# Summing the squares of the weights on VectorE before their norm products, and a rearranged last unit

## The chip, the cores and the metric

The kernel runs on one core of one Trainium2 chip. The metric is the device time of one execution in microseconds. The kernel before takes 677.63 us (median of 3 runs, 677.48 to 678.36).

## The reference

An attention over 32 memory slots feeds a feed-forward layer of two weight matrices. Cut to what matters:

```python
a = softmax(phi, axis=sequence)                     # 8 batches, 8 heads, 576 positions, 32 slots
k_m, v_m = a^T @ k, a^T @ v                         # 32 x 64 for each head
attn = softmax(q @ k_m^T / 8)                       # 576 x 32 for each head
x = (attn @ v_m)                                    # 4608 tokens x 512
h = x @ w_in                                        # 512 x 2048
out = (h - tanh(h)) @ w_out                         # 2048 x 512
```

The inputs q and k are drawn with standard deviation 20, the others as the reference has them.

## The kernel before

The fast path (`split_path`) holds w_in and w_out as pairs of float16 tiles, a high and a low part, and replaces h - tanh(h) by a short polynomial that is right for small h. Whether the inputs are small enough is checked on the chip: `stat` collects a number for each weight block and each column, `check` (L899) compares them with windows, `check_all` (L915) counts the results into `c["bad"]`, and at the end of the program every engine loads this flag (L1061) and branches (L1062) over `wide_path`, a slow general version that doesn't run here.

**Units and steps.** The 4608 tokens are 18 units of 256; the 2048 hidden columns are four blocks. After a start that is written out by hand, the loop at L844 goes through steps, one for each pair of unit and block; step number sl is 4 x unit + block and runs from 18 to 71. A step issues, in this order: the first product `mm1` of its unit and block (L540, tile hs) with its squaring on ScalarE (L547); `g1` on VectorE (L555), which reads hs; the words of list 0; `g1_square` on ScalarE (L560); on VectorE the four sums of `a_forms` (L587) for the step before and `g2` (L564); the second product `mm2_blocks` (L666 and L673) of two steps earlier; the words of list 1; `g2_high` on ScalarE (L569) and `g3` on GpSimd (L574); the words that were put off (`due`); `evict`, when a unit has been finished; the words of list 2. `in_order` (L889) then ties every instruction to the one before it on its engine, so that each engine works in exactly this order.

**The words.** Lists 0, 1 and 2 of a step are what stands ahead of ";", behind ";" and behind "|" in the entries of PLAN (L797), PLAN3 and PLAN_C (L809). For each batch PLAN places the attention work: among others "S" (scores, L246, with two transposes on VectorE, L256), "P" (`att_p`: 24 matmuls, L492, and a copy on ScalarE, L505) and "PL" (`att_pl`: the low half of that product on VectorE, L510). The entries of the batches go into a step's lists first (L817), those of PLAN_C after them (L820). The last batch has S in list 0 of steps 55 and 56, and P with PL in list 0 of steps 58, 59, 60 and 62.

**The norm products.** The check needs the sum of squares of each column of w_in and w_out. "SI" and "SO" square 2048 columns of float16 weights on ScalarE (L422, L438) into a tile of four blocks of 512 columns. "NI" and "NO" multiply these by a column of ones on TensorE: for each of four groups of 128 columns, four matmuls of one column accumulate the four blocks (L429, L447), and ScalarE copies the result (L434, L451). There are eight such products, NI0 to NI3 and NO0 to NO3, in list 2 of steps 32, 40, 48, 55, 57, 59, 61 and 63.

**PSUM.** The pool ps_a has one buffer, and all of its tiles have the tag "pa": the attention products (psc, pp), the norm products (pni, pno) and the check's product (pgood) take it in turn. hs and the sums x have their own banks, and the two output tiles o[0] and o[1] of a unit (pool ps_o) one buffer each: a new unit's first product into o[0] (L666) waits until `evict` has read the old one.

**The end of a unit.** `evict` (L715) puts the unit's output together on VectorE (L722 to L725, then L733 for each half of the tokens) and stores it (L734). For the last unit the second half goes in two pieces of 256 columns (L730), stored from two queues (L731).

Of the kernel before, what the change touches and what calls it, by code (L numbers as in the profile page):

```python
# [8 lines left out]
F32 = mybir.dt.float32  # L9
# [5 lines left out]
ALU = mybir.AluOpType  # L15
# [3 lines left out]
P = 128  # L19
# [4 lines left out]
NUNIT = B * S // UT  # L24
# [15 lines left out]
CW = (  # L40
    0.33333331252017, -0.13333128520786, 0.053934788850892, -0.021660115374759,
    0.0082189218977914, -0.0025104593252184, 0.000420695493864,
)
# [1 line left out]


V_WIN = (2.0 ** -12, 0.0025)
WI_WIN = (2.0 ** -6, 1.5)
WO_WIN = (2.0 ** -6, 3.5)
N_F1 = 32  # L50


# [260 lines left out]
def split_path(ctx, tc, c, ins, out):  # L313
    nc = tc.nc
# [6 lines left out]
    ps_a = ctx.enter_context(tc.tile_pool(name="ps_a", bufs=1, space=PSUM))  # L321
# [4 lines left out]
    wout_hi = const.tile([P, 16, DM], F16, name="wout_hi")  # L326
# [59 lines left out]
    def low(p):  # L386
        lo = low_of(p)
        for i in range(2):
            nc.vector.scalar_tensor_tensor(
                lo[:, i], tfs[p][i], S_W, his[p][:, i], op0=ALU.mult, op1=ALU.subtract  # L390
            )
# [28 lines left out]
    def squares_in(fb):  # L420
        acc["q", fb] = big.tile([P, 4, 512], F16, tag="q" if fb < 3 else "e", name=f"sqi{fb}", bufs=2 if fb < 3 else 1)
        nc.scalar.activation(acc["q", fb], win_hi[:, :, 512 * fb : 512 * fb + 512], AF.Square, scale=S_Q)  # L422

    def norms_in(fb):
        sq = acc.pop(("q", fb))
        pa = ps_a.tile([P, 2, 512], F32, tag="pa", name=f"pni{fb}")
        for k in range(4):
            for pr in range(4):
                nc.tensor.matmul(  # L429
                    pa[:, 0, k : k + 1], sq[:, pr, P * k : P * k + P], c["ones16"],  # L430
                    start=(pr == 0), stop=(pr == 3),
                )
        o = N_F1 + 2 * B + 4 * fb
        nc.scalar.activation(stat[:, o : o + 4], pa[:, 0, 0:4], AF.Copy, scale=(S_W * S_Q) ** -2)  # L434

# [4 lines left out]
    def norms_out(part):  # L440
        if part == 0:
            acc["n"] = big.tile([P, 4, 4], F32, tag="wn", name="wn", bufs=1)
        sq = acc.pop(("q", part))
        pa = ps_a.tile([P, 2, 512], F32, tag="pa", name=f"pno{part}")
        for k in range(4):
            for i in range(4):
                nc.tensor.matmul(  # L447
                    pa[:, 0, k : k + 1], sq[:, i, P * k : P * k + P], c["ones16"],
                    start=(i == 0), stop=(i == 3),
                )  # L450
        nc.scalar.activation(acc["n"][:, :, part], pa[:, 0, 0:4], AF.Copy, scale=(S_W * S_Q) ** -2)  # L451
        if part == 3:
            o = N_CHECK - 4
            nc.vector.tensor_reduce(stat[:, o : o + 4], acc["n"], axis=AX.X, op=ALU.add)
# [146 lines left out]
    acc = {}  # L601
# [50 lines left out]
    def mm2_blocks(u, fb, first, last):  # L652

        f, gg = gs.pop((u, fb))
        x = acc["x"]
        if first:
            acc[u] = [ps_o.tile([P, DM], F32, tag=f"o{i}", name=f"o{u}{fb}{i}") for i in range(2)]  # L660
        o = acc[u]
        ws = (wout_hi, wout_lo)

        def main(th):
            for k in range(4):
                nc.tensor.matmul(  # L666
                    o[th], gg[:, 0, k, P * th : P * th + P], wout_hi[:, 4 * fb + k, :], start=(first and k == 0), stop=False
                )

        def prod(dst, a, b, new=False, end=False):  # L670
            for kk in range(2):
                for n in range(2):
                    nc.tensor.matmul(  # L673
                        dst, a(1 - n, kk), b(n, kk), start=(new and kk == 0 and n == 0), stop=(end and kk == 1 and n == 1)
                    )

        def ab(th, kh):
            return lambda n, kk: gg[:, n, 2 * kh + kk, P * th : P * th + P]

        def af(i):  # L680
            return lambda n, kk: f[:, n, i, kk]

        def bb(kh, nh):
            return lambda n, kk: ws[n][:, 4 * fb + 2 * kh + kk, 256 * nh : 256 * nh + 256]

        def bf(i):
            return lambda n, kk: bts[i][:, n, fb, kk]

        lo, hi = slice(0, 256), slice(256, 512)
        m1 = (x[:, 0, lo], ab(0, 0), bb(0, 0), first)  # L690
        m2 = (o[0][:, lo], ab(0, 1), bb(1, 0))
        m3 = (o[0][:, hi], af(0), bb(1, 1))
        m4 = (o[1][:, lo], ab(1, 1), bf(3))
        m5 = (x[:, 0, hi], af(2), bf(0))
        m6 = (x[:, 1, lo], af(3), bf(1), first)
        m7 = (x[:, 1, hi], af(1), bf(2))
        if not last:
            main(0)
            main(1)
            for m in (m2, m4, m1, m5, m6, m7, m3):  # L700
                prod(*m)
            return
        sc = 1.0 / (S_G * S_W)
        ra, rb = (big.tile([P, 3, 256], F32, tag="pr", name=f"r{u}{i}") for i in range(2))
        for m, end in ((m1, False), (m5, True), (m6, False), (m7, True)):
            prod(*m, end=end)
        nc.scalar.activation(ra[:, 1], x[:, 0, lo], AF.Copy, scale=sc)
        nc.scalar.activation(rb[:, 2], x[:, 0, hi], AF.Copy, scale=sc)
        for th, ms in ((0, (m2, m3)), (1, (m4,))):
            main(th)  # L710
            for m in ms:
                prod(*m, end=m is ms[-1])
        acc["evict"] = (u, ra, rb)

    def evict():  # L715
        if "evict" not in acc:
            return
        u, ra, rb = acc.pop("evict")
        x, o, t0 = acc["x"], acc[u], u * UT
        sc = 1.0 / (S_G * S_W)  # L720
        lo, hi = slice(0, 256), slice(256, 512)
        nc.vector.scalar_tensor_tensor(ra[:, 0], x[:, 1, lo], sc, ra[:, 1], op0=ALU.mult, op1=ALU.add)  # L722
        nc.vector.scalar_tensor_tensor(rb[:, 0], x[:, 1, hi], sc, ra[:, 0], op0=ALU.mult, op1=ALU.add)
        nc.vector.tensor_tensor(ra[:, 2], ra[:, 0], rb[:, 2], op=ALU.add)
        nc.vector.tensor_tensor(rb[:, 1], rb[:, 0], rb[:, 2], op=ALU.add)  # L725
        for th, r in ((0, ra[:, 1:3]), (1, rb[:, 0:2])):
            r = r.rearrange("p a x -> p (a x)")
            if u == NUNIT - 1 and th == 1:
                for cs, q in ((hi, nc.sync), (lo, nc.scalar)):
                    nc.vector.scalar_tensor_tensor(r[:, cs], o[th][:, cs], sc, r[:, cs], op0=ALU.mult, op1=ALU.add)  # L730
                    q.dma_start(out[t0 + P :, cs], r[:, cs])  # L731
                continue
            nc.vector.scalar_tensor_tensor(r, o[th], sc, r, op0=ALU.mult, op1=ALU.add)  # L733
            nc.sync.dma_start(out[t0 + P * th : t0 + P * th + P, :], r)  # L734
# [16 lines left out]
    def two(f, g, *x):  # L751
# [15 lines left out]
        "AT": lambda b, t: att.soft_turn(b, st[b], t), "AS": lambda b, t: att_split(b, t, nc.gpsimd), "ASv": lambda b, t: att_split(b, t, nc.vector),  # L767
        "Z": warm, "P": att_p, "PL": att_pl, "H": mm1, "a": lambda u, fb: two(g1, g1_square, u, fb), "b": lambda u, fb: two(g2, g2_high, u, fb), "c": lambda u, fb: g3(u, fb, nc.gpsimd), "cv": lambda u, fb: g3(u, fb, nc.vector), "PLp": att_pl_pe,
        "T": lambda x, y: conv(10 * x + y), "L": lambda x, y: low_pool(10 * x + y), "Lv": lambda x, y: low(10 * x + y), "Lp": lambda x, y: low_pe(10 * x + y),
        "G": b_form, "SI": squares_in, "NI": norms_in, "SO": squares_out, "NO": norms_out,  # L770
        "GG": lambda: check(tc, c, big), "GX": lambda: check_all(tc, c, ps_a),
        "M": lambda u, fb: mm2(u, fb, fb in (0, 2), fb in (1, 3)), "R": load_part, "OP": save_part, "O": save,
    }
# [14 lines left out]
    first = len(nc.cur_bb.bb.instructions)  # L788
    for word in START.split():
        if ":" in word:  # L790
            k, tag = word.split(":")
# [15 lines left out]
    )  # L807

    PLAN_C = (  # L809
# [5 lines left out]
    )  # L815
    tasks = {}
    for b in range(3, B):  # L817
# [64 lines left out]
    a_forms(*forms.pop())  # L882
    for u, fb in queue:
        mm2_blocks(u, fb, fb == 0, fb == NFB - 1)
    evict()
    in_order(tc, first)

# [11 lines left out]
def check(tc, c, big):  # L899
# [4 lines left out]
    o = N_F1  # L904
    for n, (lo, hi) in ((2 * B, V_WIN), (DF // P, WI_WIN), (DM // P, WO_WIN)):
        s, g = stat[:, o : o + n], good[:, o : o + n]
# [134 lines left out]
def tile_kernel(ctx: ExitStack, tc: tile.TileContext, qt, kva, kvt, pha, phx, w_in, w_out, out):  # L1041
    nc = tc.nc
    ins = dict(qt=qt, kva=kva, kvt=kvt, pha=pha, phx=phx, w_in=w_in, w_out=w_out)
    const = ctx.enter_context(tc.tile_pool(name="const", bufs=1))
    c = {}
# [12 lines left out]
    nc.gpsimd.memset(c["beta"], BETA)  # L1058
    with ExitStack() as inner:
        split_path(inner, tc, c, ins, out)  # L1060
    bad = nc.values_load(c["bad"][0:1, 0:1], min_val=0, max_val=1)  # L1061
    with tc.If(bad > 0):  # L1062
        with ExitStack() as inner:
            wide_path(inner, tc, c, ins, out)

# [38 lines left out]
```

## Time and profile before

| | |
|---|---|
| median of 3 runs | 677.63 us |
| the profiled execution | 677.7 us |
| its span, first to last instruction | 675.9 us |
| TensorE matmuls busy | 640.8 us (95%) |
| VectorE busy | 510.7 us (76%) |
| ScalarE busy | 375.7 us (56%) |
| GpSimd busy | 256.1 us (38%) |
| norm products of w_in (L429) | 64 matmuls, 334.0 to 534.1 us |
| norm products of w_out (L447) | 64 matmuls, 549.7 to 599.5 us |
| squarings for them (L422, L438) | 8 on ScalarE, 1.89 us each |

PE is TensorE's matmuls, PEld its weight loads, DVE VectorE, ACT ScalarE, POOL GpSimd, SP the engine that issues most transfers; a q behind a name is an engine's instruction queue. A row of the timeline has start, duration, engine, line, operation, output<-input, shapes and a count of merged instructions; in square brackets stands how long the engine was idle before it and what ended that. The chain of waits is the work that ended last, followed back from the end. A row of the busy time by stretch has the stretch, its length, the busy time of PE, PEld, DVE, ACT and POOL (with instruction counts), the granted TensorE clock, the share of the DMA engines and GB/s.

### The profile page before, as it was taken

How to read it: one execution, taken by the hardware profiler on the slowest of the kernel's cores; microseconds unless marked ns; L12 is line 12 of the kernel's file. 1: busy time of each engine (PE TensorE's matmuls, PEld its weight loads, DVE VectorE, ACT ScalarE, POOL GpSimd, SP SyncE). 2: the span in 40 equal slices, each digit the busy share in tenths (PEclk: the TensorE clock that was granted, in tenths of full speed). 3: DMA queues.
4: the chain of work that ended last, by engine and by line, in shares of the span. 5: the costliest groups of instructions: out<-in, count | busy, mean ns of one | idle time of the engine just before them, and what ended most of it. 6: DMA issues, size and time to landing. Idle time of an engine off the chain costs nothing.

```text
span 675.9 us, 15441 instructions
## 1 busy us (share of the span) xinstructions
PE 640.8 (95%) x6628; PEld 447.2 (66%) x6628; DVE 510.7 (76%) x784; ACT 375.7 (56%) x506; POOL 256.1 (38%) x170
## 2 busy tenths in 40 slices
PE   4678989999999999999999999999999999999996
PEld 1336465565646567786767777777777777887874
DVE  4688999989655577965697868886888586867673
ACT  1558477765533355653565455646554587666541
POOL 0032623423111334452345344534453555455521
PEclk9979999999999999999999999999999999999999
DMA  9679663422313132214331523152415224234201
GB/s 342 265 280 363 244 180 125 172 99 86 119 63 107 60 125 72 66 62 176 102 106 42 192 80 121 49 192 68 134 49 190 72 103 121 72 118 137 77 32 37
DMA packets 26428, 86.16 MB, mean 127 GB/s; under 512 B 2928, under 2 KB 3184, under 8 KB 25584
## 3 DMA queue, kind: packets, MB, share of 16 engines
q1 hardware_dynamic: 25056, 82.87, 35.9%
q10 hardware_dynamic: 1296, 2.23, 0.9%
q8 instruction: 54, 0.88, 0.6%
q14 instruction: 22, 0.18, 0.1%
HBM read 73.55 MB, written 11.53 MB: 126 GB/s over the span
## 4 chain that ended last, share of the span: by engine, by line
PE 69%; DVE 6%; ACT 1%; DMA 1%; issue 0%; SPq 0%; DVEq 0%; ACTq 0%
PE hs L540 19%; PE o L666 12%; PE x L673 12%; PE o L673 9%; PE o L617 7%; PE h L540 2%; PE pp L492 2%; PE pkv L194 2%; DVE f L587 2%; PE o1h L617 2%; DVE h L555 1%; DVE h L564 1%; PE psc L246 1%; DMA kv<-in_kva_dram 1%; ACT u L547 1%
## 5 line engine op out<-in xcount | busy, mean ns | idle before, releaser
L574 POOL TENSOR_TENSOR g<-h,g 128x1024 f16<-128x1024 f32 x64 | 145.2, 2268 | 321.8 <-ACT g L569 212.5
L540 PEld LDWEIGHTS <-ph 128*128 128x128 f16 x2304 | 176.6, 98 | 21.9 <-issue 6.5
L540 PE MATMUL hs<-ah,ph 128*128 128x256 f16 (+3 forms) x1088 | 145.8, 248 | 0.0
L555 DVE SCALAR_TENSOR_TENSOR h<-hs,u 128x1024 f32<-128x1024 f32 x52 | 63.5, 1221 | 96.3 <-ACT u L547 96.3
L569 ACT ACTIVATE g<-h 128x1024 f16<-128x1024 f32 x72 | 76.0, 1055 | 94.8 <-DVE h L564 86.0
L540 PE MATMUL hs<-al,ph 128*128 128x256 f16 (+3 forms) x544 | 122.2, 248 | 0.0
L560 ACT ACTIVATE u<-u,beta 128x1024 f32<-128x1024 f32 x72 | 82.6, 1148 | 61.5 <-DVE h L555 61.0
L666 PE MATMUL o<-wout_hi,g 128*128 128x512 f16 x416 | 100.7, 380 | 1.5 <-DVE r L733 1.5
L564 DVE SCALAR_TENSOR_TENSOR h<-u,h 128x1024 f32<-128x1024 f32 x72 | 89.0, 1236 | 5.0 <-ACT u L560 4.6
L673 PEld LDWEIGHTS <-f 128*128 128x128 f16 x832 | 81.3, 98 | 9.5
L617 PEld LDWEIGHTS <-g 128*128 128x128 f16 x480 | 45.7, 98 | 59.4 <-issue 4.1
L547 ACT ACTIVATE u<-hs 128x1024 f32<-128x1024 f32 x52 | 53.0, 1019 | 53.1 <-PE hs L540 53.1
L617 PE MATMUL o<-wout_hi,g 128*128 128x512 f16 x256 | 78.6, 380 | 1.3 <-DVE g L574 0.8
L673 PE MATMUL x<-bt,f 128*128 128x256 f16 x624 | 76.6, 273 | 0.0
L673 PEld LDWEIGHTS <-g 128*128 128x128 f16 x624 | 60.5, 98 | 21.7 <-issue 0.8
L666 PEld LDWEIGHTS <-g 128*128 128x128 f16 x416 | 38.4, 98 | 48.5 <-issue 13.6
L587 DVE TENSOR_TENSOR f<-g 128x512 f16<-128x512 f16 x104 | 59.7, 614 | 3.9 <-POOL g L574 3.4
L540 PE MATMUL h<-ah,ph 128*128 128x256 f16 (+2 forms) x448 | 55.8, 243 | 0.0
L540 PE MATMUL h<-al,ph 128*128 128x256 f16 (+2 forms) x224 | 48.0, 242 | 1.0 <-DVE al L483 1.0
L617 PE MATMUL o<-wout_lo,g 128*128 128x512 f16 x128 | 48.6, 380 | 0.0
L510 DVE SCALAR_TENSOR_TENSOR ph<-pp,ph 128x1024 f16<-128x1024 f32 x30 | 36.5, 1216 | 1.9 <-ACT ph L505 1.7
L505 ACT ACTIVATE ph<-pp 128x1024 f16<-128x1024 f32 x32 | 32.5, 1016 | 4.0 <-PE pp L492 4.0
(134 smaller groups left out, 945.6 us busy)
## 6 DMA issues: line engine op xcount, KB each, us to landing
kv<-in_kva_dram SPq DMA_DIRECT2D x20, 516.0 KB, 4.0
q<-in_qt_dram SPq DMA_DIRECT2D x16, 576.0 KB, 4.1
chk<-in_w_in_dram SPq DMA_DIRECT2D x16, 512.0 KB, 5.2
chk<-in_w_out_dram SPq DMA_DIRECT2D x16, 512.0 KB, 3.4
out_dram<-r SPq DMA_DIRECT2D x25, 256.0 KB, 2.6
kv<-in_kva_dram SPq DMA_DIRECT2D x6, 1032.0 KB, 10.6
raws<-in_w_in_dram SPq DMA_DIRECT2D x12, 512.0 KB, 6.0
raw<-in_w_out_dram SPq DMA_DIRECT2D x12, 512.0 KB, 6.7
```

The lines of the kernel that those rows point to most:

```text
L510: nc.vector.scalar_tensor_tensor(pl, pa, S_P / (S_V * S_W), ph, op0=ALU.mult, op1=ALU.subtract)
L540: nc.tensor.matmul(hp[:, k, tu : tu + w], px[:, g, cs], d[ax][:, g, ta : ta + w], start=(n == 0), stop=(n == 5),)
L547: nc.scalar.activation(uu, hp, AF.Square, scale=1.0 / (S_A * S_P))
L555: nc.vector.scalar_tensor_tensor(h3, hp, C2 * S_G / (S_A * S_P), uu, op0=ALU.mult, op1=ALU.mult)
L560: nc.scalar.activation(uu, uu, AF.Square, bias=c["beta"])
L564: nc.vector.scalar_tensor_tensor(h3, uu, CC, h3, op0=ALU.add, op1=ALU.mult)
L569: nc.scalar.activation(gg[:, 0], h3, AF.Copy)
L574: eng.tensor_tensor(gg[:, 1], h3, gg[:, 0], op=ALU.subtract)
L587: nc.vector.tensor_tensor(o, x, y, op=op)
L617: nc.tensor.matmul(o, gx[:, k, P * tt : P * tt + P], wx[:, 4 * fb + k, :], start=(first and k == 0 and wx is wout_hi and gx is gh), stop=( ...
L666: nc.tensor.matmul(o[th], gg[:, 0, k, P * th : P * th + P], wout_hi[:, 4 * fb + k, :], start=(first and k == 0), stop=False)
L673: nc.tensor.matmul(dst, a(1 - n, kk), b(n, kk), start=(new and kk == 0 and n == 0), stop=(end and kk == 1 and n == 1))
```

## The change

- A new word "SS" (`squares_sum`) sums the four blocks of squares into the first, in two float16 sums on VectorE. It stands in list 1 of the steps in which the norm product stood.
- `norms_in` and `norms_out` multiply only that first block: 4 matmuls in place of 16. Their words move from list 2 of a step to the end of list 0 of the next one: NI0 to NI3 to steps 33, 41, 49 and 56, NO0 to NO3 to steps 58, 60, 62 and 64.
- The windows of the check for w_in and w_out are drawn in by about 0.2%.
- For the last unit, the upper 256 columns of its second half of tokens get a tile h1 of their own in ps_a, and `main` issues that half as two runs of 256 columns, h1 first. `evict` makes the sum rb[:,1] (L725) for that unit only after the first half's L733, evicts h1 and then the rest, and stores both with one transfer from ScalarE's queue.
- The flag is loaded (`values_load`) ahead of the last `evict` and not at the end of the program.

```diff
-WI_WIN = (2.0 ** -6, 1.5)
-WO_WIN = (2.0 ** -6, 3.5)
+WI_WIN = (1.002 * 2.0 ** -6, 1.497)
+WO_WIN = (1.002 * 2.0 ** -6, 3.493)
...
+    def squares_sum(i):
+
+        sq = acc["q", i]
+        nc.vector.tensor_tensor(sq[:, 0:2], sq[:, 0:2], sq[:, 2:4], op=ALU.add)
+        nc.vector.tensor_tensor(sq[:, 0], sq[:, 0], sq[:, 1], op=ALU.add)
+
     def norms_in(fb):
...
-            for pr in range(4):
-                nc.tensor.matmul(
-                    pa[:, 0, k : k + 1], sq[:, pr, P * k : P * k + P], c["ones16"],
-                    start=(pr == 0), stop=(pr == 3),
-                )
+            nc.tensor.matmul(pa[:, 0, k : k + 1], sq[:, 0, P * k : P * k + P], c["ones16"], start=True, stop=True)
...
         def main(th):
+            if th and u == NUNIT - 1:
+                for dst, cs, end in ((acc["h1"], hi, last), (o[1][:, lo], lo, False)):
+                    for k in range(4):
+                        nc.tensor.matmul(
+                            dst, gg[:, 0, k, P : 2 * P], wout_hi[:, 4 * fb + k, cs],
+                            start=(first and k == 0), stop=(end and k == 3),
+                        )
+                return
...
+        if first and u == NUNIT - 1:
+            acc["h1"] = ps_a.tile([P, 2, 512], F32, tag="pa", name="oh")[:, 0, lo]
...
-        nc.vector.tensor_tensor(rb[:, 1], rb[:, 0], rb[:, 2], op=ALU.add)
         for th, r in ((0, ra[:, 1:3]), (1, rb[:, 0:2])):
+            if th == (u == NUNIT - 1):
+                nc.vector.tensor_tensor(rb[:, 1], rb[:, 0], rb[:, 2], op=ALU.add)
...
-                for cs, q in ((hi, nc.sync), (lo, nc.scalar)):
-                    nc.vector.scalar_tensor_tensor(r[:, cs], o[th][:, cs], sc, r[:, cs], op0=ALU.mult, op1=ALU.add)
-                    q.dma_start(out[t0 + P :, cs], r[:, cs])
+                for cs, p in ((hi, acc["h1"]), (lo, o[1][:, lo])):
+                    nc.vector.scalar_tensor_tensor(r[:, cs], p, sc, r[:, cs], op0=ALU.mult, op1=ALU.add)
+                nc.scalar.dma_start(out[t0 + P :, :], r)
...
-(31, "CW CE SI0"), (32, "CW CW | NI0"),
+(31, "CW CE SI0"), (32, "CW CW ; SS0"),
...
-(55, "CW CW CQ CQ | NI3"), (56, "CW CW CQ CQ SO0"), (57, "CW CW CQ CQ | NO0"), (58, "CW CQ SO1"),
+(55, "CW CW CQ CQ ; SS3"), (56, "CW CW CQ CQ SO0"), (57, "CW CW CQ CQ ; SS0"), (58, "CW CQ SO1"),
...
+(33, "NI0"), (41, "NI1"), (49, "NI2"), (56, "NI3"), (58, "NO0"), (60, "NO1"), (62, "NO2"), (64, "NO3"),
...
+    c["wide"] = nc.values_load(c["bad"][0:1, 0:1], min_val=0, max_val=1)
     evict()
     in_order(tc, first)
...
-    bad = nc.values_load(c["bad"][0:1, 0:1], min_val=0, max_val=1)
-    with tc.If(bad > 0):
+    with tc.If(c["wide"] > 0):
```

More of the change, by code (lines that the diff above doesn't have):

```diff
@@ L445, in norms_out @@
         for k in range(4):
[L446 to L450, printed above, removed]
+            nc.tensor.matmul(pa[:, 0, k : k + 1], sq[:, 0, P * k : P * k + P], c["ones16"], start=True, stop=True)
         nc.scalar.activation(acc["n"][:, :, part], pa[:, 0, 0:4], AF.Copy, scale=(S_W * S_Q) ** -2)
@@ L769, in split_path @@
         "T": lambda x, y: conv(10 * x + y), "L": lambda x, y: low_pool(10 * x + y), "Lv": lambda x, y: low(10 * x + y), "Lp": lambda x, y: low_pe(10 * x + y),
-        "G": b_form, "SI": squares_in, "NI": norms_in, "SO": squares_out, "NO": norms_out,
+        "G": b_form, "SI": squares_in, "NI": norms_in, "SO": squares_out, "NO": norms_out, "SS": squares_sum,
         "GG": lambda: check(tc, c, big), "GX": lambda: check_all(tc, c, ps_a),
```

10 rows, old and new, of the table PLAN_C are left out of this document.

## The prediction

> **What bounds the kernel now.** I read the page first, then the busy time by stretch, then the chain of waits in order of time around the norm products, then VectorE's timeline beside it, and last the instructions at the flag's load and at the final store.
>
> ```profile
> span 675.9 us, 15441 instructions
> PE 69%; DVE 6%; ACT 1%; DMA 1%; issue 0%; SPq 0%; DVEq 0%; ACTq 0%
> 540.00:610.00 70.00, 70.00 (x788) 55.67 (x786) 51.36 (x80) 50.77 (x73) 35.16 (x25) 1.00 0.35 109
> ```
>
> The profiled execution took 677.7 us, 1.8 us more than its span; the median of the runs is 677.63. In the stretch with the norm products of w_out, TensorE is busy for all of its 70.00 us at full granted clock (1.00), VectorE for 51.36. So here what TensorE issues less is time gained, and what makes it wait is time lost, one for one. The chain shows where the products stand:
>
> ```profile
> 533.90 0.38 PE pni L429 x16
> 534.28 2.64 PE hs L540 x24
> 536.92 0.65 PE psc L246 x16
> 537.57 1.83 PE o L666 x8
> ...
> 549.86 0.38 PE pno L447 x16
> 550.24 2.64 PE hs L540 x24
> 552.88 0.77 PE pp L492 x24
> 553.65 1.84 PE o L666 x8
> ...
> 566.83 0.38 PE pno L447 x16
> ...
> 569.91 0.78 PE pp L492 x24
> 570.68 1.83 PE o L666 x8
> ...
> 583.04 0.38 PE pno L447 x16
> ...
> 586.12 0.77 PE pp L492 x24
> 586.89 1.83 PE o L666 x8
> ...
> 599.24 0.38 PE pno L447 x16
> ...
> 602.26 1.73 PE o L666 x8
> ```
>
> Columns: start, duration, what. A norm product (pni, pno) is 16 matmuls in 0.38 us, at the end of a step, ahead of the next step's first product (hs). Behind hs come the attention products (psc, pp) and then, with no gap, the second product (o, L666). psc, pp, pni and pno are all tiles of tag "pa" in pool ps_a, which has one buffer. In the old order a whole hs stands between a norm product and the next user of that buffer.
>
> **What the change takes away.** Twelve of 16 matmuls go: 0.38 x 12/16 = 0.28 us for each of the eight, 2.3 us in all if nothing else moved. The thresholds of the check are constants and cost nothing.
>
> **What it moves: the order on "pa".** The list of step 56 puts the attention words first (the loop over b fills it before PLAN_C does), so TensorE now issues hs, psc, NI3, then L666; in steps 58, 60 and 62 it issues hs, pp, NO0/NO1/NO2, then L666. The norm product must wait until the last reader of psc or pp is done with the buffer, and L666, which needs none of it, is queued behind it. The trace has such a wait at the start, where one pp follows another:
>
> ```profile
> 47.43 0.41 PE L492 MATMUL pp<-win_hi,vh 64*32 64x512 f16 x8 [1.11 <-ACT ph L519]
> ```
>
> TensorE stood 1.11 us until ScalarE had read the pp before. In the moved places the last reader is on VectorE: for psc the two transposes (L256), for pp the subtraction that makes its low half (L510):
>
> ```profile
> 539.22 0.84 DVE L256 STREAM_TRANSPOSE sc<-psc 128x288 f32<-128x288 f32 x2
> 550.27 1.22 DVE L564 SCALAR_TENSOR_TENSOR h<-u,h 128x1024 f32<-128x1024 f32 x1
> 552.86 1.28 DVE L733 SCALAR_TENSOR_TENSOR r<-o,r 128x512 f32<-128x512 f32 x2
> 554.06 1.21 DVE L555 SCALAR_TENSOR_TENSOR h<-hs,u 128x1024 f32<-128x1024 f32 x1
> 555.19 1.22 DVE L510 SCALAR_TENSOR_TENSOR ph<-pp,ph 128x1024 f16<-128x1024 f32 x1
> 572.20 1.21 DVE L510 SCALAR_TENSOR_TENSOR ph<-pp,ph 128x1024 f16<-128x1024 f32 x1
> 588.41 1.22 DVE L510 SCALAR_TENSOR_TENSOR ph<-pp,ph 128x1024 f16<-128x1024 f32 x1
> ```
>
> Today nobody waits for these readers: they end 2.5 to 2.8 us after TensorE has gone on to L666 (540.06 against 537.57; 556.41 against 553.65; 573.41 against 570.68; 589.63 against 586.89).
>
> **What it adds on VectorE.** One squares_sum is an f16 sum of 1024 columns and one of 512. The nearest rows:
>
> ```profile
> L587 DVE TENSOR_TENSOR f<-f,g 128x512 f16<-128x512 f16 x52 | 22.7, 436 | 0.0
> L599 DVE TENSOR_TENSOR bt<-wout_hi 128x2048 f16<-128x2048 f16 x2 | 2.4, 1222 | 0.0
> ```
>
> 512 columns take 0.44 us and 2048 take 1.22, so 1024 take 0.44 + 0.78 x 512/1536 = 0.70, and the pair 1.1 us. From above it is bounded by the slower passes quoted, 1.22 for 1024 columns (L564) and half of 1.28 for 512 (L733): 1.9. I take 1.1, since the L587 and L599 rows are the same operation on the same type. The sum is issued behind L564. Where the step ends without an eviction, VectorE idles before its next L555 anyhow and the sum is hidden (steps 32, 40, 48, 55, 59, 63). In steps 57 and 61 the eviction is queued behind it, then L555 and L510 without a gap: 554.06, 555.19 follow on the end of the eviction at 554.14. There the whole chain goes 1.1 us later.
>
> **The sum.** Each of the four bad places is: end of the last reader after the change, plus some 0.14 us for the signal and four matmuls (0.10 = 0.38 x 4/16), against the old start of L666. Where the chain on VectorE hangs on hs it comes 0.38 earlier, as the norm product ahead of hs is gone.
> - Step 56: 540.06 - 0.38 + 0.14 = 539.82 against 537.57: +2.25.
> - Step 58: 556.41 + 1.1 + 0.14 = 557.65 against 553.65: +4.0.
> - Step 60: 573.41 - 0.38 + 0.14 = 573.17 against 570.68: +2.5.
> - Step 62: 589.63 + 1.1 + 0.14 = 590.87 against 586.89: +4.0.
>
> Together +12.7. In step 58 and 62 I don't take 0.38 off, since there VectorE is busy without a gap from L564 on. None of it is given back: TensorE has no idle time in these steps, and the other engines, which the pause lets catch up, do not end the steps. On ScalarE the copy of the norm product now stands ahead of L560 and waits with it, but L560 feeds L564, which has the four L587 ahead of it on VectorE and comes hardly later.
>
> In steps 33, 41, 49 and 64 no attention product stands ahead, the sums end well before hs does, and each gives 0.28 to 0.38: -1.2.
>
> **The last unit.** Splitting main's second half into columns 256 to 511 and 0 to 255 gives 32 matmuls of 256 columns for 16 of 512. hs takes 2.64/24 = 0.110 for 256 columns, L666 1.83/8 = 0.229 for 512: two halves cost what the whole did, and their doubled weight loads lie beside the matmuls. The tile h1 takes "pa" when its last user, the check's product, is long read. At the end:
>
> ```profile
> 669.81 0.76 DVE L730 SCALAR_TENSOR_TENSOR r<-o,r 128x256 f32<-128x256 f32 x2 [0.20 <-PE o L673]
> 670.60 0.37 ACTq L731 DMA_DIRECT2D out_dram<-r  x1
> L1061 ACTq TENSOR_LOAD <-bad x1: 616/616/616, 671.0 to 671.0; - x1
> L1062 ACTq COMPARE_BRANCH x1: 54/54/54, 671.7 to 671.7; - x1
> L1062 ACTq EVENT_SEMAPHORE  x1: 17/17/17, 674.7 to 674.7; - x1
> ```
>
> Today both half evictions wait for the last matmul, then ScalarE's queue issues the store (0.37), loads the flag (0.62), branches at 671.7, and comes out of the branch 3.0 us later; that signal at 674.7 is the latest such row. After the change one half is evicted under the matmuls (0.76/2 less), and the flag was loaded before: the branch comes up to 1.0 us sooner. Against it, one store of 128x512 replaces two of 128x256 on two queues and may land later, and another engine may be late next. I take -0.8, between -1.0 and +0.4. The flag load itself stands ahead of the evictions on VectorE and ScalarE, which then wait for TensorE anyhow.
>
> Sum: 12.7 - 1.2 - 0.8 = +10.7. From 677.7 this gives 688.4 us.
>
> **The rivals.**
> (a) The pauses also cost clock. The pauses in steps 58 and 62 are 4.2 us long (553.27 to 557.5). The nearest that the trace has:
>
> ```profile
> 29.41 1.98 PE L194 MATMUL pkv<-kv,e 128*32 128x129 f32 x64 [3.02 <-ACT e L180]
> 39.11 0.63 PE L492 MATMUL pp<-win_hi,vl 64*32 64x512 f16 x8 [2.12 <-DVE vl L466]
> 36.00:46.00 10.00, 7.29 (x56) 2.17 (x56) 8.49 (x19) 3.89 (x6) 4.63 (x4) 0.66 0.70 229
> 26.00:36.00 10.00, 4.62 (x122) 2.84 (x120) 5.75 (x13) 3.21 (x8) 0.00 (x0) 1.00 0.41 148
> ```
>
> Around 26 to 36 a wait of 3.02 us left the granted clock at 1.00; from 36 to 46, around a wait of 2.12 us and a nearly idle TensorE before it, it fell to 0.66. That is 7.29 x 0.34 = 2.5 to 10 x 0.34 = 3.4 us, about 3, for one such event. The two pauses of about 2.6 us should not do it, each of the two long ones may: 691.4 with one event, 694.4 with two. The Trainium skill ("TensorE: Matmul & The Clock Gate", Part 1, What's actually happening) has the clock halve after an idle window of about 3.4 us that runs free of the program. By that rule a pause of 4.2 us holds a whole idle window in about (4.2 - 3.4)/3.4, a quarter, of its positions (an estimate from that page), and the sum would be 688.4 or 691.4. The trace agrees in that 3.02 us of idle kept the clock; its fall around a shorter wait does not fit so simply.
>
> (b) The norm products do not wait for "pa", because the buffer is handed on otherwise than I read it. Then eight savings remain, but in steps 58 and 62 the evictions, 1.1 us later, hold L666: the first eviction ends at 552.86 + 0.64 + 1.1 = 554.60 against 553.65, +0.95, and the same in 62. Six times -0.28, +1.9, and -0.8 at the end: -0.6, 677.1, which is no change. For it: nothing in the trace; against it, the 1.11 us wait.
>
> (c) The change does what it saves on paper: no wait on "pa", the sums hidden everywhere. 8 x -0.28 - 0.8 = -3.0: 674.7, faster. It needs VectorE idle behind L564 in steps 57 and 61, and the rows from 552.86 to 556.41 show it full.
>
> (d) The pauses are there but the sums cost nothing in 57 and 61: 2.2 less and some 0.4 for hs, 685.8. Or the sums cost 1.9: 690.0.
>
> **How the numbers follow.** My forecast (pauses, clock kept, with (d) as its edges) has 0.60, (a) 0.25, (b) 0.06, (c) 0.09. The predicted time is 688.4. The range runs from 685.5, the lower edge of (d), to 692.5, which takes in one clock event with its spread: it leaves out (b), (c) and most of two events, just under 0.2. A difference of 0.2% is 1.4 us, about the least that a measurement here tells from no change. Faster is (c), 0.09; same is (b), 0.06; slower is the rest, 0.85.
>
> **What would show it.** In the profile after: TensorE waits ahead of L429 (NI3) for the transposes of L256, some 2.5 us once, and ahead of the norm product in L448 or so (NO0 to NO2) for L510, 4.2, 2.6 and 4.2 us; no wait before the other four products; pni and pno with 4 matmuls in 0.1 us; VectorE's new sums at about 0.7 and 0.4 us; the granted clock still 1.00 between 540 and 625 (if lower, (a)); ScalarE's flag load gone from the end. If TensorE shows no wait there and the stretch is not longer, the reading of "pa" was wrong; if the pauses are there and the total is not longer, then TensorE was not what ended these steps.

## The result and the profile after

The changed kernel takes 699.93 us (median of 6 runs, 698.08 to 700.72) against 677.57 (6 runs, 676.73 to 678.82): ratio 1.0322, 95% interval 1.0304 to 1.0339, slower by 22 us. Forecast were 10.7 us more, at most 15. The profiled execution has a span of 697.8 us, 21.9 more than before. Two slow runs among those below, one of the kernel before (693.55 us) and one of the partly filled kernel (1719.99 us), count in none of the ratios.

From the page after, TensorE's waits and the busy time of two stretches (stretch, its length, busy time of TensorE's matmuls, weight loads, VectorE, ScalarE, GpSimd, then the granted clock):

```profile
PE 56%; DVE 14%; ACT 3%; DMA 2%; issue 2%; SPq 0%; DVEq 0%; ACTq 0%
PE pno L448 <- DVE ph L508: 13.3, 3, 5.5
PE pni L434 <- DVE sc L256: 2.5, 1, 2.5
540.00:610.00 70.00, 55.90 (x549) 39.89 (x550) 47.41 (x74) 39.20 (x57) 26.94 (x19) 0.87 0.29 90
563.90:568.00 4.10, 4.10 (x14) 1.68 (x12) 3.10 (x6) 4.01 (x8) 0.37 (x1) 0.50 0.65 231
```

VectorE has more than doubled its share of the chain (6 to 14%). TensorE waits three times for L508 (L510 before) ahead of NO0, NO1 and NO2, 13.3 us together, and once for the transposes ahead of NI3: the four waits of the forecast, two of them longer. The last two lines hold what the forecast lacked: between 540 and 610 the clock is 0.87, and right behind the second wait, while TensorE is busy all the time, it is 0.50. The chain of waits after, at the four places and at NO3:

```profile
540.01 0.77 DVE sc L256 x2
540.82 0.26 PE pni L434 x4
541.09 3.30 PE o L672 x8
...
562.52 1.14 DVE ph L508
563.71 0.25 PE pno L448 x4
563.95 3.44 PE o L672 x8
...
584.15 1.14 DVE ph L508
585.34 0.25 PE pno L448 x4
585.59 3.24 PE o L672 x8
...
606.63 1.14 DVE ph L508
607.82 0.24 PE pno L448 x4
608.06 3.44 PE o L672 x8
...
625.14 0.08 PE pno L448 x4
625.22 1.75 PE o L672 x8
```

Each of the first four norm products starts when VectorE has finished, and the eight matmuls behind it (L672, L666 before) take 3.2 to 3.4 us; where there was no wait, at NO3, they take 1.75.

The first product hs starts every step on TensorE, so its starts show where time is lost:

| hs of step | before | after | later by |
|---|---|---|---|
| 33 | 334.37 | 334.08 | -0.29 |
| 35 | 350.28 | 350.39 | 0.11 |
| 45 | 436.24 | 436.20 | -0.04 |
| 46 | 446.52 | 447.18 | 0.66 |
| 55 | 524.77 | 525.88 | 1.11 |
| 57 | 542.30 | 547.28 | 4.98 |
| 59 | 558.38 | 570.65 | 12.27 |
| 61 | 575.41 | 591.72 | 16.31 |
| 63 | 591.61 | 614.89 | 23.28 |
| 71 | 652.64 | 675.47 | 22.83 |

Steps 55 and 56 cost 3.9 us (forecast 2.25), 57 and 58 cost 7.3 (4.0), 59 and 60 cost 4.0 (2.5), 61 and 62 cost 7.0 (4.0); ahead of them 1.1 is lost where 0.9 was to be gained, behind them 0.4 is gained, and the end gains 0.9 (22.83 to 21.9).

VectorE's and GpSimd's timelines around the eviction of step 57:

```profile
554.96 0.68 DVE L427 TENSOR_TENSOR sqo<-sqo 128x1024 f16<-128x1024 f16 x1
555.67 0.42 DVE L428 TENSOR_TENSOR sqo<-sqo 128x512 f16<-128x512 f16 x1
556.47 0.42 DVE L731 SCALAR_TENSOR_TENSOR r<-x,r 128x256 f32<-128x256 f32 x1
556.60 2.14 POOL L572 TENSOR_TENSOR g<-h,g 128x1024 f16<-128x1024 f32 x1 [5.96 <-ACT g L567]
556.81 2.21 DVE L732 TENSOR_TENSOR r<-r,r 128x256 f32<-128x256 f32 x1
558.69 2.40 POOL L414 TENSOR_TENSOR fy<-chk 128x512 f32<-128x512 f32 x2
558.94 1.25 DVE L735 TENSOR_TENSOR r<-r 128x256 f32<-128x256 f32 x1
```

The sums cost 0.68 and 0.42 us, as forecast. But the eviction's two additions L732 and L735 take 2.21 and 1.25. Before they were L724 and L725, and GpSimd started its next instruction only at 552.66:

```profile
552.20 0.41 DVE L724 TENSOR_TENSOR r<-r,r 128x256 f32<-128x256 f32 x1
552.53 0.42 DVE L725 TENSOR_TENSOR r<-r 128x256 f32<-128x256 f32 x1
```

In the changed kernel L732 ends when GpSimd's L572 does: the sums have moved the eviction into GpSimd's work.

At the end ScalarE's store, branch and last signal, with its flag load now ahead of them:

```profile
693.55 0.38 ACTq L740 DMA_DIRECT2D out_dram<-r  x1
L894 ACTq TENSOR_LOAD <-bad x1: 467/467/467, 689.6 to 689.6; - x1
L1071 ACTq COMPARE_BRANCH  x1: 54/54/54, 694.0 to 694.0; - x1
L1071 ACTq EVENT_SEMAPHORE  x1: 17/17/17, 697.0 to 697.0; - x1
```

Before, 1.1 us lay between the start of that store and the branch; now it is 0.45, and again 3.0 us pass to the signal.

### The profile page after: what moved, and what is told of

Same layout as the page of the kernel before. It is cut to its first block, busy times and chain, and to the rows that moved or that the text cites. A ratio compares the mean times of both kernels' runs of the same rounds, so it can differ in the third digit from the quotient of the medians.

```text
span 697.8 us, 15305 instructions
## 1 busy us (share of the span) xinstructions
PE 646.4 (93%) x6548; PEld 449.1 (64%) x6548; DVE 527.0 (76%) x800; ACT 375.7 (54%) x506; POOL 256.8 (37%) x170
## 4 chain that ended last, share of the span: by engine, by line
PE 56%; DVE 14%; ACT 3%; DMA 2%; issue 2%; SPq 0%; DVEq 0%; ACTq 0%
PE hs L538 15%; PE o L672 10%; PE x L679 9%; PE o L615 7%; PE o L679 7%; DVE f L585 3%; DVE h L553 3%; DVE h L562 2%; DMA kv<-in_kva_dram 2%; PE h L538 2%; PE pp L490 2%; ACT u L545 2%; PE pkv L194 2%; PE o1h L615 1%; ACT sqi L422 1%
## 5 line engine op out<-in xcount | busy, mean ns | idle before, releaser
L572 POOL TENSOR_TENSOR g<-h,g 128x1024 f16<-128x1024 f32 x64 | 144.9, 2265 | 335.3 <-ACT g L567 239.5
L672 PE MATMUL o<-wout_hi,g 128*128 128x512 f16 x400 | 103.4, 399 | 2.3 <-DVE r L742 2.3
L562 DVE SCALAR_TENSOR_TENSOR h<-u,h 128x1024 f32<-128x1024 f32 x72 | 89.0, 1236 | 5.3 <-ACT u L558 4.6
L679 PEld LDWEIGHTS <-f 128*128 128x128 f16 x832 | 81.3, 98 | 9.5
L615 PE MATMUL o<-wout_hi,g 128*128 128x512 f16 x256 | 78.5, 379 | 1.4 <-DVE g L572 0.8
L679 PE MATMUL x<-bt,f 128*128 128x256 f16 x624 | 76.6, 273 | 0.0
L679 PEld LDWEIGHTS <-g 128*128 128x128 f16 x624 | 61.1, 99 | 22.2 <-issue 2.6
L672 PEld LDWEIGHTS <-g 128*128 128x128 f16 x400 | 38.2, 101 | 49.6 <-issue 19.5
L585 DVE TENSOR_TENSOR f<-g 128x512 f16<-128x512 f16 x104 | 57.6, 594 | 3.9 <-POOL g L572 3.4
L508 DVE SCALAR_TENSOR_TENSOR ph<-pp,ph 128x1024 f16<-128x1024 f32 x30 | 36.4, 1214 | 1.9 <-ACT ph L503 1.7
```

Of the source, the lines that this page charges most:

```text
L508: nc.vector.scalar_tensor_tensor(pl, pa, S_P / (S_V * S_W), ph, op0=ALU.mult, op1=ALU.subtract)
L562: nc.vector.scalar_tensor_tensor(h3, uu, CC, h3, op0=ALU.add, op1=ALU.mult)
L572: eng.tensor_tensor(gg[:, 1], h3, gg[:, 0], op=ALU.subtract)
L585: nc.vector.tensor_tensor(o, x, y, op=op)
L615: nc.tensor.matmul(o, gx[:, k, P * tt : P * tt + P], wx[:, 4 * fb + k, :], start=(first and k == 0 and wx is wout_hi and gx is gh), stop=( ...
L672: nc.tensor.matmul(o[th], gg[:, 0, k, P * th : P * th + P], wout_hi[:, 4 * fb + k, :], start=(first and k == 0), stop=False)
```

## The experiments

Theory A: the loss is the wait for the one buffer of "pa", a TensorE that comes out of such a wait at half clock, and a chain on VectorE that the sums push into GpSimd's work. Rivals: contention alone makes the products behind the waits slow; the sums cost time wherever they stand; part of the loss is in the last unit.

**Filling the pauses.** The edit, in the changed kernel (Dxyz is xy matmuls; with z = 1 they overwrite x, otherwise they add to it):

```diff
+    def dummy(n, new):
+        for _ in range(n):
+            nc.tensor.matmul(acc["x"][:, 0], c["nid16"], c["zero16"]..., start=bool(new), stop=bool(new))
...
-(56, "NI3"), (58, "NO0"), (60, "NO1"), (62, "NO2"),
+(56, "D100 NI3"), (58, "D221 NO0"), (60, "D110 NO1"), (62, "D211 NO2"),
```

> The changed kernel with matmuls that add zeros to the sums x (or are overwritten there) issued ahead of NI3, NO0, NO1 and NO2: 10, 22, 11 and 21 of 512 columns, which fill the four pauses at full clock nearly to their ends. Theory A (a paused TensorE loses clock, 1.4 to 2.1 us after each pause, 7.0 in all): the products after the pauses take 1.83 us and not 3.3 to 3.4, granted clock 0.99, 692.9 us against 699.9. Theory B (they are slow for another reason, such as contention when all engines start again): still 3.3 us each, 700 us.

Measured: ratio 1.0211 (1.0185 to 1.0237), 692.0 us beside 677.7. Its busy time over the whole stretch and one place of its chain:

```profile
530.00:640.00 110.00, 107.55 (x1009) 79.06 (x1008) 77.63 (x118) 64.42 (x93) 49.93 (x36) 1.00 0.31 97
560.81 0.24 PE pno L448 x4
561.05 1.75 PE o L672 x8
```

The products behind all four places take 1.75 us and the clock is 1.00 throughout. Of the 22 us, 8 go with the filled pauses, 7.3 of them between steps 55 and 63; so clock is the larger part of the 11.6 us that were not foreseen. It comes from TensorE standing still, since the other engines do what they did: the additions of step 57 take 2.20 and 1.25 us beside GpSimd here too.

**Filling only the first part of the pauses.** The same with `D050`, `D161`, `D070` and `D151`.

> The run with the filled pauses again, but with 5, 16, 7 and 15 matmuls of zeros, which leaves the last 1.3, 1.9, 1.2 and 1.7 us of the four pauses open. Theory A (what costs clock is a pause of some 2.5 us or more; where 2.5 did and 1.3 doesn't): clock kept behind all four, 692 us as with the filled pauses. Theory B (any gap ahead of the products costs clock): 3.3 us for the product behind at least two of the four pauses, 695 us or more.

Measured: 692.4 us, ratio 1.0214 (1.0193 to 1.0236). TensorE's timeline at step 58, the longest open pause:

```profile
559.25 3.63 PE L757 MATMUL x<-zero,nid 128*128 128x512 f16 x16
564.79 0.24 PE L448 MATMUL pno<-ones,sqo 128*128 128x1 f16 x4 [1.91 <-DVE ph L508]
564.89 1.89 PE L672 MATMUL o<-wout_hi,g 128*128 128x512 f16 x8
```

These four pauses of 1.2 to 1.9 us cost no clock. From step 55 to step 63 its profile loses 14.83 us and that of the filled run 14.84, and the times agree within the intervals, as A expected.

**The order alone.** The kernel before with the words at the changed places, 16 matmuls, no sums:

```diff
-(55, "CW CW CQ CQ | NI3"), ... (57, "CW CW CQ CQ | NO0"), ... (59, "CW CQ | NO1"), ...
+(55, "CW CW CQ CQ"), ... (57, "CW CW CQ CQ"), ... (59, "CW CQ"), ...
+(33, "NI0"), (41, "NI1"), (49, "NI2"), (56, "NI3"), (58, "NO0"), (60, "NO1"), (62, "NO2"), (64, "NO3"),
```

> The kernel before with the norm products at the changed places, but of 16 matmuls as before and without the sums on VectorE; end as before. Theory A (buffer wait plus clock; the sums add only to steps 58 and 62): four pauses of 2.5 to 2.8 us, each followed by half clock worth 1.4 to 2.0, 10.8 + 0.5 + 6.4: about 695 us; the additions ahead of the eviction in steps 57 and 61 take 0.41 us again. Theory B (half of the loss comes from the sums' contention on VectorE): 688 us.

Measured: 695.12 us, ratio 1.0257 (1.0230 to 1.0283), the 695 of theory A. TensorE's waits, and the product behind the second one:

```profile
PE pno L447 <- DVE ph L510: 8.4, 3, 2.8
PE pni L429 <- DVE sc L256: 2.5, 1, 2.5
559.25 0.56 PE pno L447 x16
559.82 3.23 PE o L666 x8
```

With no sum and no saving the order alone costs 17 of the 22 us: pauses of 2.5 to 2.8 us, all four followed by half clock (behind the fourth it begins only with the fifth of the eight matmuls). The additions of step 57 take 0.42 us each again.

**The eviction's additions from PSUM.** In the changed kernel:

```diff
-        nc.scalar.activation(rb[:, 2], x[:, 0, hi], AF.Copy, scale=sc)
-        nc.vector.tensor_tensor(ra[:, 2], ra[:, 0], rb[:, 2], op=ALU.add)
+        nc.vector.scalar_tensor_tensor(ra[:, 2], x[:, 0, hi], sc, ra[:, 0], op0=ALU.mult, op1=ALU.add)
...
-                nc.vector.tensor_tensor(rb[:, 1], rb[:, 0], rb[:, 2], op=ALU.add)
+                nc.vector.scalar_tensor_tensor(rb[:, 1], x[:, 0, hi], sc, rb[:, 0], op0=ALU.mult, op1=ALU.add)
```

> The changed kernel with the two additions of the eviction (L732, L735), which read two tiles of SBUF, made from the sum x in PSUM and one tile of SBUF; the same result, the same order, one copy on ScalarE less in each unit. Theory A (in steps 57 and 61 the additions took 2.2 and 1.2 us in place of 0.41, because GpSimd was running and both read a second SBUF tile): 0.4 us each with GpSimd still running, L508 and the norm product 2.3 us sooner in step 58 and about 2 in step 62, 695.7 us against 699.9. Theory B (they are slow for another reason, such as a wait for ScalarE or for TensorE's sums): they stay at 2 us or the time goes to the next instruction, 700 us.

Measured: 692.52 us, ratio 1.0216 (1.0196 to 1.0235). The two additions in step 57 and GpSimd beside them:

```profile
556.10 2.13 POOL L572 TENSOR_TENSOR g<-h,g 128x1024 f16<-128x1024 f32 x1 [5.46 <-ACT g L567]
556.58 0.41 DVE L731 SCALAR_TENSOR_TENSOR r<-x,r 128x256 f32<-128x256 f32 x1
556.91 0.41 DVE L734 SCALAR_TENSOR_TENSOR r<-x,r 128x256 f32<-128x256 f32 x1
...
603.63 0.24 PE L448 MATMUL pno<-ones,sqo 128*128 128x1 f16 x4 [2.79 <-DVE ph L508]
603.73 1.89 PE L672 MATMUL o<-wout_hi,g 128*128 128x512 f16 x8
```

With GpSimd at work the additions take 0.41 us: what held them goes when one of their inputs is in PSUM. The Trainium skill ("GPSIMD Engine Reference", Specifications) says that GpSimd shares its SBUF interfaces with VectorE, with contention for instructions of two SBUF inputs; these rows agree. The time fell by 7.4 us and not by the 4 expected, and the rest is mostly clock: the last of its four pauses, 2.79 us, kept it (1.89 us behind it), and the clock is halved for 13.7 us in these steps, for 20.5 in the changed kernel.

The traces show why. In all ten profiles the granted clock changes only on a grid of 3.41 us, which lies otherwise in each of them. Of the windows of this grid at full clock, all 33 in which TensorE idles for more than 2.0 us (the window less its busy time) are followed by half clock (ten of them are at the program's end), none with less than 1.9 is, and of the seven between three are. The 2.79 us lie across two windows here, 0.84 and 1.96 us; the same pause of step 60 has 2.02 in one window, and half clock follows. The wait of 3.02 us at the start, on which the prediction relied, shows it too (busy time by stretch; first two rows the kernel before, last two the kernel with filled pauses):

```profile
24.81:28.23 3.42, 1.58 (x6) 0.58 (x4) 1.70 (x3) 1.23 (x3) 0.00 (x0) 1.00 0.68 275
28.23:31.64 3.41, 2.23 (x80) 1.89 (x80) 0.00 (x0) 1.13 (x1) 0.00 (x0) 1.00 0.02 5
25.57:28.98 3.41, 0.94 (x36) 0.95 (x40) 1.19 (x3) 1.24 (x2) 0.00 (x0) 1.00 0.49 197
28.98:32.39 3.41, 2.50 (x56) 1.65 (x44) 0.74 (x4) 0.00 (x0) 0.00 (x0) 0.50 0.02 5
```

Before, the wait splits into 1.84 and 1.18 us of idle and costs nothing; in the other kernel 2.47 us of it fall into one window, and the clock halves. It does so in three of the ten profiles.

**The norm products ahead of the attention words.** In the changed kernel the four words move to the head of the list:

```diff
-    tasks = {}
+    tasks = {56: ["NI3"], 58: ["NO0"], 60: ["NO1"], 62: ["NO2"]}
```

> The changed kernel with NI3, NO0, NO1 and NO2 at the head of their list, ahead of the attention product of the step and not behind it. Then psc or pp waits for ScalarE's copy of the norm product, which stands behind the squaring of hs (1.0 us) and takes 0.17: four pauses of 1.2 to 1.3 us. Theory A (a pause costs clock only when it is long, 2.5 us did): clock kept, four times 1.25 less four times 0.28 saved, evictions 1.1 later without harm, end -0.9: about 680.5 us. Theory B (any pause of TensorE over about 1 us costs clock): 6 more, 686 us.

Measured: 684.81 us, ratio 1.0116 (1.0097 to 1.0134): between the two. Its waits in the stretch and the busy time:

```profile
PE o L672 <- DVE r L742: 4.0, 3, 1.4
PE pp L490 <- ACT wn L449: 3.5, 3, 1.2
530.00:640.00 110.00, 101.40 (x1008) 79.80 (x1007) 84.14 (x125) 69.30 (x100) 54.37 (x39) 1.00 0.33 107
```

The clock stays at 1.00 and the waits for the copy are 1.2 us, as A has it. What A's sum missed is the first line: the evictions of steps 57 and 61, pushed into GpSimd's work by the sums, hold the second product for 1.36 and 1.25 us. The third wait of that line, some 30 us further on, stands in the kernel before too (1.04 us).

**The last unit alone.** The change's last hunks (flag load, h1, split main, one store) on the kernel before.

> Only the last unit's part of the change: the flag loaded ahead of the last eviction, h1 with its split main, one final store; sums, norm products and windows as before. Theory A (the whole loss lies in the moved norm products, the end gains): the end is 0.9 us shorter, 676.7 us against 677.6. Theory B (the early flag load or the split main holds something up, and part of the loss is there): 678 us or more.

Measured: 677.4 us beside 677.7, ratio 0.9998 (0.9984 to 1.0011). The timing can't tell 0.9 us. In its profile hs of step 71 starts 1.0 us earlier than before, which stems from the start (1.2 earlier already in step 18), and the span is 1.9 shorter, 674.0: the last 0.9 is the end's.

**The change for w_in alone.** NI0 to NI2 with their sums on the kernel before:

```diff
-(32, "CW CW | NI0"), ... (40, "CW CW | NI1"), ... (48, "CW CW | NI2"),
+(32, "CW CW ; SS0"), (33, "NI0"), ... (40, "CW CW ; SS1"), (41, "NI1"), ... (48, "CW CW ; SS2"), (49, "NI2"),
```

> The kernel before with the change for w_in alone and only for NI0, NI1 and NI2 (sums in steps 32, 40 and 48, four matmuls in list 0 of steps 33, 41 and 49, the drawn-in window); NI3, w_out and the end as before. The prediction's view (each gives 0.28 to 0.38): steps from 50 on start 0.9 to 1.1 us sooner, 676.6 us against 677.6. Theory A (the end of VectorE's eviction in steps 33, 41 and 49 hangs on GpSimd and not on TensorE's first product, so L666 of the next step starts when it did): the first product of steps 33, 41 and 49 starts 0.4 us sooner, that of steps 35, 43 and 51 as before; 677.6 us.

Measured: 678.54 us, ratio 1.0021 (1.0011 to 1.0031): slightly slower. In its profile hs of step 33 starts 0.37 sooner than before and that of step 35 0.03 later; step 41 0.40 sooner than step 40 had left it, step 43 back at the old lag: theory A. TensorE's wait for the eviction ahead of L666 (L672 here) grows from 0.2 to 0.5 us. What it didn't expect is 0.8 us at step 46 (446.52 before, 447.24 here), where TensorE waits inside pkv for a load:

```profile
445.85 1.08 PE L194 MATMUL pkv<-kv,e 128*32 128x129 f32 x28 [0.61 <-DMA kv<-in_kva_dram]
L124 SPq DMA_DIRECT2D kv<-in_kva_dram x2: 328/778/1227, 440.0 to 440.5; - x2
```

One of the two issues of that load took 1.23 us, 0.38 before. All six profiles with sums for w_in lose 0.70 to 0.84 us between steps 45 and 46 and wait 0.5 to 0.6 us for this load; the three without lose 0.17 to 0.35 and have no such wait. The long issue is not what it takes: with the norm products ahead of the attention words the loss is 0.82 and the issues last 0.33 and 0.38. Why sums that end some 36 us ahead of the load do that is open.

**The norm products where "pa" is free.** The list of the version (NI0 to NI2 as before the change; the tiles of sqo0 and sqo2 in the buffer "qt"):

```diff
...
+(55, "CW CW CQ CQ ; SS3"), ... (56, "| NI3"), (58, "; SS0"), (59, "| NO0"), (60, "; SS1"), (61, "| NO1"),
+(62, "; SS2"), (63, "| NO2"), (64, "; SS3"), (65, "| NO3"),
...
```

> The change with its norm products put where the buffer of tag pa is free: NI3 at the end of step 56, NO0 to NO3 at the ends of steps 59, 61, 63 and 65, their sums in list 1 of steps 55, 58, 60, 62 and 64, none of which has an eviction; two of the square tiles in another buffer of SBUF; NI0 to NI2 as before the change (16 matmuls, no sum). Theory A (the loss is the wait for the buffer, the clock after it and the sum ahead of an eviction): no wait of TensorE at a norm product, clock 0.99, five savings of 0.28 and 0.9 at the end, 675.3 us. Theory B (the sums on VectorE cost time wherever they stand): 678 us or more, with longer waits for VectorE in steps 58 to 65.

Measured: 676.19 us, ratio 0.9983 (0.9969 to 0.9997): just faster than the kernel before, by some 1.2 us and not 2.3; the interval ends close to 1. No wait at a norm product, the clock at 1.00. Its waits between 530 and 640, and one sum:

```profile
PE o L677 <- ACT u L550: 1.3, 1, 1.3
PE o L677 <- DVE r L747: 0.4, 1, 0.4
PE pp L495 <- ACT wn L454: 0.2, 1, 0.2
560.58 2.28 DVE L428 TENSOR_TENSOR sqo<-sqo 128x512 f16<-128x512 f16 x1
```

Each norm product still puts its step's end 0.3 us ahead (hs of step 60 starts 0.51 sooner than before, that of 59 only 0.20), and the step behind gives it back (step 61 0.21, 62 0.52, 63 0.25) while TensorE waits for VectorE or ScalarE. Its hs of step 71 is 0.23 us sooner than before; the rest is the end. The second sum above took 2.28 us, 0.42 in the changed kernel: GpSimd's L577 runs from 560.45 to 562.58 beside it, and this sum too has its inputs in SBUF. Of the versions run, only this one is faster than the kernel before, by 0.2%.

## Why the prediction was wrong

The direction and the mechanism were right: the order on "pa" makes TensorE wait at exactly the four places named, and the order alone costs 17 us. The size was half of what came.

- **Clock, the step that failed.** Rival (a) gave one or two events, at the two long pauses, and said that "the two pauses of about 2.6 us should not do it". All four pauses were followed by half clock: the eight matmuls took 3.30 - 1.83, 3.44 - 1.83, 3.24 - 1.83 and 3.44 - 1.83 longer, 6.1 us, and the next products of steps 58 and 62 some 0.9 more (the L679 groups behind took 1.24 and 1.37 for 0.87). The filled pauses took it away, 692 for 700. The evidence relied on, a 3.02 us wait at the start that kept the clock, was luck of position: it lies across two windows of the grid, and in three other profiles the same wait lost the clock. In steps 55 to 66 of the runs above, ten pauses of 2.5 to 2.8 us lost it nine times and twelve of 1.2 to 1.9 us never; at the start, where two waits of 1.35 and 2.12 us share a window, it goes as well (the fall to 0.66 that the prediction could not place). What counts is some 2 us of idle in one window of 3.41 us and not a whole idle window. By that a pause of 4.2 us always loses it (at least 2.1 us lie in one window), where the prediction's estimate had a quarter, and one of 2.6 us loses it in some 60% of its positions (an estimate from the grid: (3.41 + 2.6 - 2 x 1.95)/3.41). The forecast had the price of an event, 3 us, too high and its chance far too low.
- **The sums' 1.1 us.** Their own cost was right. L508 of step 58 ends 563.66 - 547.28 = 16.38 us behind hs of step 57, before 556.41 - 542.30 = 14.11: 2.3 later where 1.1 was forecast; in step 62 it is 1.8. In step 58 the sums add 1.1 and the two additions 2.6, while the instruction ahead of them (L562, L564 before) starts 1.4 sooner after hs of step 57. The sum treated VectorE's queue as a shift by 1.1 and didn't ask what GpSimd does at the new time. With the additions from PSUM the distance is 13.7.
- **"Each gives 0.28 to 0.38" in steps 33, 41 and 49.** It gave nothing: TensorE's first product is early, but L666 of the next step waits for an eviction whose a_forms hang on GpSimd. The chain view showed that before (f, L587, 2.27 us in the chain at 339.53), and it was not read for this term. In the changed kernel 1.1 us are lost for the 0.9: 0.7 at the kv load of step 45, 0.4 at that of step 53 (a wait of 0.38 us), whose cause is open as well.
- **The four pauses themselves** were forecast at 2.5, 4.2, 2.6 and 4.2 us and came at 2.5, 5.5, 2.8 and some 5.
- **The last unit.** -0.8 forecast, -0.9 by the starts of hs, read as the flag load and one half eviction off the tail.
- **Rivals (b) and (c)** fell with the waits. (c) has more against it: with free buffers the savings in steps 59 to 63 are given back, and 0.23 us of them are left at step 71; the full 2.3 us did not come in any run.

## What to carry to other kernels

Before a step is moved on an in-order engine, list who holds its buffer at the new place; a product that needs one buffer of a ring of one stops everything queued behind it. Price a new pause of TensorE of 2.5 us or more as the pause plus 1.5 to 2 us at half clock, and look whether matmuls can fill all but its last 1 to 2 us; one old pause that kept the clock proves little, since the next may fall otherwise on the grid. When VectorE's work is shifted, check what GpSimd runs at the new time: here instructions with two inputs in SBUF were held until it was done.

## What the runs showed of the hardware

- After a pause of 2.5 us TensorE ran at half clock for one window of 3.41 us (540.71 to 544.12), after the two of 5.0 and 5.5 us for two windows. The Trainium skill ("TensorE: Matmul & The Clock Gate", Part 1, What's actually happening) has the clock halve after an idle window of about 3.4 us that is free-running: the grid and the pause of 2.8 us without loss agree with it, but a whole idle window was not needed, as some 2 us of idle in one were enough.
- Matmuls that add zeros keep the clock as others do (64 of them, clock 1.00).
- VectorE's addition of 256 columns from two SBUF tiles took 0.41 us with GpSimd idle, up to 2.21 with GpSimd running, and 0.41 with GpSimd running and one input in PSUM.
- ScalarE comes out of the branch over the general version 3.0 us after it (694.0 to 697.0), VectorE 3.2 (692.8 to 696.0). ScalarE is the last here: with the flag load no longer between its store and its branch, that stretch fell from 1.1 to 0.45 us.
